# Sorted attention with a feed-forward block: the last three pairs' scatters and loads at other steps, pair 11 put back two rows a slot, and two other moves

## The chip, the cores and the metric

The kernel runs on one core of a Trainium2 chip. The metric is the device time of one execution in microseconds (us), and the number given for a kernel is the median of its runs. One execution of each kernel is profiled; its page and its trace show the engines TensorE (PE for matrix products, PEld for the loading of its weights), VectorE (DVE), ScalarE (ACT), GpSimd (POOL), and SyncE (SP), whose queue issues most of the DMAs ("SPq").

## The reference, cut to what matters

The inputs are `q`, `k` and `v` of 4 batches x 8 heads x 768 tokens x 64, and 16 centroids per head. Each query and each key belongs to the centroid it is most similar to, and a query sees only the keys of its own cluster. The result, with the heads side by side, is the input of a feed-forward block with 512 inputs and 2048 hidden features.

```python
q_assign = np.argmax(np.einsum('bhsd,hcd->bhsc', q_n, c_n), axis=-1)
k_assign = np.argmax(np.einsum('bhsd,hcd->bhsc', k_n, c_n), axis=-1)
mask = q_assign[:, :, :, None] == k_assign[:, :, None, :]
scores = np.where(mask, scale * np.matmul(q, k.transpose(0, 1, 3, 2)), -1e9)
attn = softmax(scores)
x = np.matmul(attn, v)            # then (B, H, S, D) -> (B*S, H*D)
h = x @ w_in
g = np.maximum(h, 0.0) + alpha * np.minimum(h, 0.0)
return g @ w_out
```

All is in float32.

## The kernel before

**Pairs, steps and slots.** Two heads are worked on together: 16 pairs `n`, four to a batch. Pairs 0 to 3 (n < `NCH` = 4) take the clusters into the scores by a second matmul; from pair 4 on a mask on DVE does it; and pairs 9 to 15 (n >= `NO` = 9) are sorted by cluster first ("ordered"), so that each chunk of 128 keys needs only a window of the queries. The program is written out by hand, in a fixed order, as a list of steps `u`. Each pair (or half of its queries) has three steps (`SB` = 3). A first loop runs to step 23 and a second from `TOGETHER` = 24 to step 75 (`NS`). In the second loop the pairs begin at these steps: 9 at 48, 10 at 51, 11 at 54, the two halves of pair 8 at 57 and 60, then 12 at 63, 13 at 66, 14 at 69 and 15 at 72. A step has five slots (`SLOTS`); in a first step of a pair the first three are taken by the two halves of its scores (L784 matmuls, exponentials L802 and L805) and by the weighing of the pair before (`weigh` L939, `weigh_near` L972), and only slots 3 and 4 are left.

**What fills a slot.** A slot issues, in this order: what `later` has put off to this tick (`tick`), one piece of the pair's own sums and masks (`mask` L825), possibly some scatters, then pieces of the feed-forward block of an earlier batch (`feed`), then what `prep_at` holds for the step and slot. A feed-forward piece is a hidden block of 128 features (`hidden`: L1066 matmuls, the copy L1072 on ACT, the slope L1058 on DVE, issued with the next piece) or a quarter of an output tile (`final`: L1084 matmuls; L1090, L1092 its end). Hidden and final products take their banks from `ps_f`, of two buffers; all small products share the one bank of `misc()`. The last batch's feed-forward block is another form, seven products in place of eight (`last_pieces`: `hidden` L1244, its copies L1176 and additions L1179, its `slopes` L1184; `final` L1300); there `g_sums` (L1223) and `w_out_sums` (L1232) form sums of the operands on DVE.

**The way of an ordered pair.**
- At step `ORDERS[n - NO]`, `load(n)` issues eight DMAs from `q` and `k` into two tiles of the pool `inp`, which has four buffers (`load_v`, L141, does the same for `v` of pairs that are not ordered). One and two steps later `order_features` (two transposes, L567) and `order_sims` (four matmuls, L575) follow, and behind these the counting on DVE (`order_counts`), `order_begins` (L601), `order_ranks` (L609 to L611) and `order_rows`, each put off by some ticks.
- `order_rows` puts the pair's scattering into the list `sorting`: six stages, each a load of 128 tokens of one head (`order_stage`, three DMAs on SP's queue, L661) and four scatters (`order_scatter`, an indirect DMA each on POOL's queue, L675, plus at the first of a stage a copy of token numbers). There are only two stage tiles, so that a stage's load waits until the scatters of the stage two before have read it. "13.2" is stage 2 of pair 13.
- How many scatters a slot issues is said by `scatters_at(v, s, i)`, where `v` is the step counted from 48. Ahead of them `pace` issues a token: a copy of one element on ACT (L651), which POOL reads by a copy (L652). So POOL keeps to the slots of ACT; tokens are in the pool `pace`, of eight buffers.
- `order_load(n)` reads the sorted pair back: two DMAs for the token numbers (L688), eight for queries and keys (L697), two for the values (L706), all on SP's queue. It stands in the program before the step of its start by a lead of 4, 3, 3, 4, 4, 4 and 3 steps for pairs 9 to 15.
- `prep_clusters` (L444, its copy L448) and `prep_keys` come four steps ahead of the pair's start, `order_blocks` (two transposes, L713) and `order_queries` (L719) in the step before it.
- Behind its last step: `invert` (L907) and `normalise_near` (L978). Then the result is turned to rows in two parts (`to_rows`, three transposes on PE, L1002, and a copy on ACT, L1005), and `put_back` scatters the 12 rows to their tokens, each with a token of `pace` (L1011). `fetch_back` reads the result (four DMAs on SP's queue, L1023) and `turn_back` (L1030, two transposes on DVE) puts it into the input of the feed-forward block. This is spread over slots: parts begin 6 and 12 ticks after `normalise_near`, a row a slot, and `turn_back` comes 7 ticks after `fetch_back`. Only pair 15 has its parts at 6 and 9, two rows a slot, and `turn_back` 4 ticks on.

**Queues.** Each engine, and SP as the issuer of DMAs, takes its instructions in the program's order. On SP's queue thus stand, one behind the other, `load`, `load_v`, `order_stage`, `order_load`, `fetch_back` and the stores of the output.

**The pairs 0 to 3.** `prep_argmax` leaves the clusters of a pair as rows of `member`, and `of_heads`, put off by 12 ticks for pair 0 and by 8 for the others, issues the copies for the second matmul: `prep_queries` (DMAs on ACT's queue, L476) and two activations (L431).

Of the kernel before, what the change touches and what calls it, by code (L numbers as in the profile page):

```python
# [23 lines left out]
def kernel(  # L24
# [70 lines left out]
    def later(slots, piece):  # L95
        due.setdefault(now[0] + slots, []).append(piece)
# [8 lines left out]
    NO = WHOLE * NCH - 3  # L105
    NP = len(pairs)
# [309 lines left out]
    def prep_argmax(n, ps):  # L416
        top, first, pieces = argmax(ps, exact=n < NCH)
        for piece in pieces:
            piece()
        firsts[n] = first  # L420
        if n >= NCH:
            return
        member = memp.tile([P, HS], BF16, name="member")
        outside = memp.tile([P, 2, HS], BF16, name="outside")
        nc.vector.transpose(out=member, in_=top.rearrange("p t c -> p (t c)"))

        def of_heads():
            if n > 0:
                prep_queries(n, 0, 0)
            for h in range(2):  # L430
                nc.scalar.activation(  # L431
                    out=outside[HP:P, h, :], in_=member[HP:P, :], func=AF.Identity,
                    scale=pick[HP:P, h:h + 1], bias=pick[HP:P, h + 2:h + 3])

        members[n] = member, outside
        later(12 if n == 0 else 8, of_heads)

    def prep_clusters(n):

# [286 lines left out]
    SB = NJ // GROUP  # L726
# [248 lines left out]
    def normalise_near(n):  # L975
        outT = inp.tile([P, 2, NJ, D], FP32, name="qk").rearrange("p h j d -> p (h j d)")
        for side in range(2):
            nc.vector.tensor_tensor(out=outT[:, side * HS:(side + 1) * HS],  # L978
                                    in0=pos.pop((n, side))[:, 0:HS],
                                    in1=rds.pop((n, side)), op=ALU.mult)  # L980
        whole = tc.dram_tile([2 * S, D], FP32, name=f"back{n}")
        to = dram_disjoint_views(whole, 2 * NJ)
        found = orders.pop(n)
        place = found[:, :, :, 0]
        nc.vector.tensor_scalar(out=place, in0=place, scalar1=0, scalar2=S - 1,
                                op0=ALU.max, op1=ALU.min)
        rows = [sorts["byrow"].tile([P, HJ, P], FP32, name=f"rows{i}") for i in range(2)]

        dense = n == NP - 1
        starts = (6, 9) if dense else (6, 12)  # L990
        for i in range(2):
            later(starts[i], lambda i=i: to_rows(outT, rows, i))
            for x in range(NJ):
                later(starts[i] + 2 + (x // 2 if dense else x),
                      lambda i=i, x=x: put_back(to, place, rows, i * NJ + x))
        later(starts[1] + 2 + (HJ if dense else NJ), lambda: fetch_back(n, whole))
# [19 lines left out]
    def fetch_back(n, whole):  # L1016

        b, hp = pairs[n]
        raw = inp.tile([P, 2, NJ, D], FP32, name="qk").rearrange("p h j d -> p (h j d)")
        for h in range(2):  # L1020
            for x in range(D // Q):
                r = h * D + x * Q
                nc.sync.dma_start(  # L1023
                    out=raw[r:r + Q, :].rearrange("p (t i) -> p t i", i=Q),
                    in_=whole[h * S:(h + 1) * S, x * Q:(x + 1) * Q].rearrange(
                        "(t p) i -> p t i", p=Q))

        def turn_back():
            for half in range(2):
                nc.vector.transpose(out=x_tile(b, half)[:, hp, :],  # L1030
                                    in_=raw[:, half * HS:(half + 1) * HS])
        later(4 if n == NP - 1 else 7, turn_back)

    def x_tile(b, half):
        if (b, half) not in xTs:
# [73 lines left out]
    KH, NQ, HC = NCH // 2, NF // 2, DM // 2  # L1109
# [32 lines left out]
    def last_pieces():  # L1142
# [75 lines left out]
        def g_sums(x):  # L1218
            (t0, t1), (z0, z1) = g[x][0], g[NQ + x][0]
            S1, S2, S4 = (g_sum(x, m) for m in ("S1", "S2", "S4"))  # L1220
            for to, p, q, op in ((S1, t1, z1, ALU.add), (S2, S1, t0, ALU.subtract),
                                 (t1, t0, t1, ALU.subtract), (S4, z0, S2, ALU.subtract)):
                nc.vector.tensor_tensor(out=to, in0=p, in1=q, op=op)  # L1223

        def w_out_sums(x):

            T1, T2, T3, T4 = (w_out_form(m, x) for m in ("T1", "T2", "T3", "T4"))
            B11, B12, B21, B22 = (
                w_out_sb[:, f, c0:c0 + HC].rearrange("p (a w) -> p a w", a=KH)
                for f in (x, NQ + x) for c0 in (0, HC))  # L1230
            for to, p, q in ((T1, B12, B11), (T2, B22, T1), (T3, B22, B12), (T4, B21, T2)):
                nc.vector.tensor_tensor(out=to, in0=p, in1=q, op=ALU.subtract)  # L1232

        late = deque()
# [101 lines left out]
            return [p1, p5, p6, p2, p7, p3, p4]  # L1336

        def room_for_y():
            late.popleft()()
            t = sorts["xmore"].tile([P, NCH, HS], FP32, name="xT").rearrange(  # L1340
                "p c q -> p (c q)")
            ys.extend(ypool.tile([P, DM], FP32, name="y") for _ in range(HJ))
            ys.extend(t[:, i * DM:(i + 1) * DM] for i in range(HJ))
            for x in (NQ - 2, NQ - 1):
                g_sums(x)
            for x in (NQ - 2, NQ - 1):
                w_out_sums(x)
        pieces = []
        for x in range(NQ):
            pieces += hidden(x)  # L1350
# [15 lines left out]
    FREE = SLOTS * SB - 3  # L1366


    ORDERS = [26, 29, 35, 38, 41, 56, 59]
    prep_at, load_at = {}, {}  # L1370
    for (n, half), u in start_of.items():
        def at(step, slot, piece):
            prep_at.setdefault((step, slot), []).append(piece)
        if half is None:
            t = ORDERS[n - NO]
            load_at.setdefault(t, []).append(lambda n=n: load(n))
            for i in range(2):
                at(t + 1, FIRST + i, lambda n=n, i=i: order_features(n, i))
            at(t + 2, 2, lambda n=n: order_sims(n))
            load_at.setdefault(u - (3 if n in (NO + 1, NO + 2, NP - 1) else 4), []).append(  # L1380
                lambda n=n: order_load(n))
            at(u - 4, 0, lambda n=n: prep_clusters(n))
            for i in range(2):
                at(u - 1, i, lambda n=n, i=i: order_blocks(n, i))
                at(u - 1, FIRST + i, lambda n=n, i=i: order_queries(n, i))
            continue
        if half == 0:
            if n < NCH:
                if n > 1:
                    load_at.setdefault(max(u - 7, 0), []).append(lambda n=n: load(n))  # L1390
                if n > 0:
                    load_at.setdefault(max(u - 6, 0), []).append(lambda n=n: load_v(n))
            else:
                load_at.setdefault(u - 9, []).append(lambda n=n: load(n))
                load_at.setdefault(u - 7, []).append(lambda n=n: load_v(n))
            if n < NCH:
                for g in range(len(groups)):
                    at(u - 4, FIRST + g, lambda n=n, g=g: prep_features(n, g))
            else:
                for w in range(2):  # L1400
                    at(u - 7, FIRST + w + (u - 7 == TOGETHER - 1),
                       lambda n=n, w=w: prep_blocks(n, w))
            at(u - (3 if n < NCH else 5 if u - 6 < TOGETHER else 6), FIRST,
               lambda n=n: prep_sims(n)) if u - 6 < 2 * TOGETHER else at(
                   u - 6, FIRST + 1, lambda n=n: prep_sims(n))
            if n >= NCH:
                at(u - 4, FIRST if u - 4 < TOGETHER else 0, lambda n=n: prep_clusters(n))
        if n < NCH:

            if half == 1 or n == 0:  # L1410
                at(u - (3 if half else 1), FIRST,
                   lambda n=n, half=half: prep_queries(n, half, 0))
            continue
        for h in range(2):
            at(u - 1, FIRST + h, lambda n=n, half=half, h=h: prep_queries(n, half, h))
# [4 lines left out]
    def scatters_at(v, s, i):  # L1420


        if v < SB:
            return 1 + (s == 0 or i == 0)
        if v < 3 * SB:
            return 0
        if v < 4 * SB:
            return int(s == 0 or i % 2 == 0)
        return 1 + (s == 0 or i % 2 == 0)

    def feed(pieces):
        for _ in range(pieces):
# [27 lines left out]
    for u in range(-AHEAD, TOGETHER):  # L1460
        for piece in load_at.get(u, []):
            piece()
        n, half, s = steps[max(u, 0)]
# [51 lines left out]
    for u in range(TOGETHER, NS + 1):  # L1515
        for piece in load_at.get(u, []):
            piece()
        if u < NS:
            n, half, s = steps[u]
        if s == 0 or u == NS:  # L1520
# [16 lines left out]
            if prior[1] is None:  # L1537
                normalise_near(prior[0])
            else:
                normalise(*prior)  # L1540
# [276 lines left out]
```

## Time and profile before

| what | value |
|---|---|
| median of three runs | 941.22 us |
| lowest and highest | 939.76 and 941.53 us |
| the profiled execution's own time | 941.51 us |
| its span in the trace | 939.6 us |
| mean granted clock of TensorE | 0.997 |
| matmuls, and instructions in all | 3963 and 11988 |
| L1066, hidden products of three batches | x768, 258.9 us, 490 ns each |
| L1084, final products of three batches | x576, 254.8 us, 596 ns each |
| L1011, rows put back | x84, 85.7 us, 1021 ns each |
| L1072, ACT's copies of hidden blocks | x96, 46.0 us, 479 ns each |

The span runs from the first to the last instruction; 1.9 us of the profiled execution's time lie around it. The page gives for each engine the time in which it was busy, and for each group of instructions its line, engine and tile, the count, the busy time and the mean of one, and then the engine's idle time just ahead of them with what ended most of it ("<-"). The busy time of the engines, stretch by stretch, of which the second loop is from 244 us on and the last batch's feed-forward block from about 750 us on:

| us of the span | PE | DVE | ACT | POOL | granted clock | DMA share |
|---|---|---|---|---|---|---|
| 0 to 100 | 94.03 | 74.97 | 59.70 | 31.07 | 1.00 | 0.50 |
| 100 to 244 | 144.00 | 125.38 | 51.06 | 25.65 | 1.00 | 0.54 |
| 244 to 440 | 195.39 | 157.00 | 49.85 | 114.56 | 1.00 | 0.33 |
| 440 to 545 | 100.75 | 85.75 | 31.20 | 70.19 | 0.98 | 0.53 |
| 545 to 662 | 113.42 | 82.67 | 27.52 | 86.78 | 1.00 | 0.53 |
| 662 to 750 | 88.00 | 45.69 | 18.75 | 32.81 | 1.00 | 0.18 |
| 750 to 860 | 109.35 | 68.86 | 19.72 | 21.21 | 1.00 | 0.08 |
| 860 to 940 | 74.14 | 15.86 | 4.96 | 0.00 | 0.98 | 0.06 |

### The profile page before, as it was taken

The numbers are of one execution on the slowest core, as the hardware profiler recorded it, in microseconds if no ns is written. First come the engines' busy times: TensorE is split into PE (matmuls) and PEld (weight loads), VectorE is DVE, ScalarE is ACT, GpSimd is POOL, SyncE is SP. The second block draws the span as 40 slices with busy tenths as digits, with TensorE's granted clock in tenths as the row PEclk, the third lists the DMA queues.
The fourth block names the chain that finished last, engine by engine and source line by source line (L and its number), as shares of the span: only waits on it lengthen the run. The fifth ranks groups of instructions, "written<-read, shape, count | busy, mean of one in ns | idle before, by whom it ended". The sixth has DMA issues, their size and how long they took to land.

```text
span 939.6 us, 11988 instructions
## 1 busy us (share of the span) xinstructions
PE 919.1 (98%) x3963; PEld 495.3 (53%) x3963; DVE 656.2 (70%) x1246; ACT 262.8 (28%) x661; POOL 382.3 (41%) x580
## 2 busy tenths in 40 slices
PE   8999999999999999999999999999999999999997
PEld 5534444445455454454544544555555555556886
DVE  5797798799679589598987889754647135598100
ACT  5764444323023132231212332122212120221000
POOL 2333222200026677478575786668533471000000
PEclk9999999999999999999999999999999999999999
DMA  8433758039002635252952383662501012000000
GB/s 298 135 117 98 144 131 150 18 62 196 1 9 72 156 82 137 62 120 76 176 100 41 59 138 73 149 124 60 92 31 27 12 37 53 1 0 1 23 23 25
DMA packets 226708, 77.71 MB, mean 83 GB/s; under 512 B 210752, under 2 KB 214544, under 8 KB 226640
## 3 DMA queue, kind: packets, MB, share of 16 engines
q1 hardware_dynamic: 217728, 62.72, 30.9%
q0 software_dynamic: 8064, 13.78, 4.7%
q8 instruction: 33, 0.54, 0.2%
q10 hardware_dynamic: 848, 0.39, 0.2%
q14 instruction: 35, 0.29, 0.1%
HBM read 52.25 MB, written 24.25 MB: 81 GB/s over the span
## 4 chain that ended last, share of the span: by engine, by line
PE 82%; DVE 10%; SPq 3%; DMA 1%; issue 1%; POOL 1%; ACT 1%; DVEq 0%; POOLq 0%; ACTq 0%
PE fps L1084 24%; PE fps L1066 22%; PE sps L784 6%; PE vps L939 5%; PE sps L1244 4%; PE sps L1300 4%; PE vps L1244 2%; PE vps L1300 2%; PE fps L784 2%; SPq L697 1%; PE mps L972 1%; PE fps L1300 1%; PE fps L1244 1%; PE vps L972 1%; SPq L127 1%
## 5 line engine op out<-in xcount | busy, mean ns | idle before, releaser
L1066 PE MATMUL fps<-xT,w_in_sb 128*128 128x384 f32 x768 | 258.9, 490 | 0.0
L1084 PE MATMUL fps<-w_out_sb,gT 128*128 128x512 f32 x576 | 254.8, 596 | 2.5 <-DVE gT L1058 2.5
L675 POOL DMA_INDIRECT scratch<-stage,off x168 | 177.9, 1059 | 75.1 <-issue 29.6
L1066 PEld LDWEIGHTS fps<-xT,w_in_sb 128*128 128x128 f32 x768 | 142.5, 190 | 103.1 <-issue 4.3
L1084 PEld LDWEIGHTS fps<-w_out_sb,gT 128*128 128x128 f32 x576 | 107.4, 190 | 134.8 <-issue 121.4
L1072 ACT COPY gT<-fps 128x384 f32<-128x384 f32 x96 | 46.0, 479 | 236.2 <-PE fps L1066 236.2
L652 POOL COPY paced<-pace 1x1 f32<-1x1 f32 x205 | 51.2, 250 | 139.5 <-ACT pace L651 138.9
L1058 DVE SCALAR_TENSOR_TENSOR gT<-gT,alpha 128x384 f32<-128x384 f32 x96 | 61.2, 647 | 58.7 <-ACT gT L1072 58.5
L1011 POOL DMA_INDIRECT back<-rows,off x84 | 85.7, 1021 | 24.2 <-issue 18.6
L784 PE MATMUL sps<-qkT 64*128 64x384 f32 (+1 forms) x464 | 86.1, 490 | 0.4 <-DVE qkT L713 0.4
L805 ACT ACTIVATE E<-sps 128x768 f32<-128x768 f32 (+1 forms) x76 | 56.3, 786 | 62.6 <-PE sps L793 38.4
L784 PEld LDWEIGHTS sps<-qkT 64*128 64x128 f32 x464 | 41.8, 188 | 39.7 <-issue 14.6
L825 DVE SCALAR_TENSOR_TENSOR more<-aq,key,more 128x384 f32<-128x384 bf16 (+2 forms) x116 | 60.4, 577 | 0.0
L939 PE MATMUL vps<-E,vt 128*64 128x384 f32 x292 | 54.2, 495 | 1.5 <-DVE xT L1042 1.5
L271 POOL TENSOR_TENSOR w_in_sb<-w_in_sb,power 128x512 f32<-128x512 f32 x16 | 25.7, 1612 | 68.6 <-DVE w_in_sb L268 68.6
L825 DVE SCALAR_TENSOR_TENSOR E<-aq,key,E 128x384 f32<-128x384 bf16 (+2 forms) x88 | 45.3, 569 | 0.6 <-ACT E L802 0.6
L271 POOL TENSOR_TENSOR w_out_sb<-w_out_sb,power 128x512 f32<-128x512 f32 x16 | 22.5, 1412 | 56.0 <-DVE w_out_sb L268 56.0
L907 DVE RECIPROCAL inverses<-mps 64x12 f32<-64x12 f32 (+1 forms) x42 | 10.5, 249 | 48.1 <-PE mps L894 47.9
L835 DVE TENSOR_TENSOR acc<-acc,E 128x768 f32<-128x768 f32 x35 | 33.3, 951 | 14.6 <-ACT E L805 13.6
L1090 ACT COPY y<-fps 128x512 f32<-128x512 f32 x18 | 10.6, 587 | 102.3 <-PE fps L1084 102.3
L1092 DVE TENSOR_TENSOR y<-y,fps 128x512 f32<-128x512 f32 x24 | 16.3, 680 | 28.5 <-PE fps L1084 28.5
L805 ACT ACTIVATE more<-sps 128x768 f32<-128x768 f32 (+1 forms) x40 | 29.2, 764 | 12.5 <-PE sps L784 11.6
(284 smaller groups left out, 1178.4 us busy)
## 6 DMA issues: line engine op xcount, KB each, us to landing
raw<-in_moe_w_in_dram SPq DMA_DIRECT2D x16, 512.0 KB
raw<-in_moe_w_out_dram SPq DMA_DIRECT2D x16, 512.0 KB
out_dram<-y SPq DMA_DIRECT2D x21, 256.0 KB
qk<-scratch SPq DMA_DIRECT2D x56, 96.0 KB
qk<-in_q_dram SPq DMA_DIRECT2D x48, 96.0 KB
qk<-in_k_dram SPq DMA_DIRECT2D x48, 96.0 KB
w_in_kept<-w_in_sb SPq DMA_DIRECT2D x8, 512.0 KB
vt<-in_v_dram SPq DMA_DIRECT2D x9, 384.0 KB
```

What stands on the lines that cost most here:

```text
L652: nc.gpsimd.tensor_copy(out=sorts["paced"], in_=token)
L675: nc.gpsimd.indirect_dma_start(out=scratch[n][1][h * NX + xx], out_offset=bass.IndirectOffsetOnAxis(ap=ranks[n][:, xx, h:h + 1], axis=0), ...
L784: nc.tensor.matmul(out=bank(ps, h, m), lhsT=qkT[r:r + D, S + c * P:S + (c + 1) * P], rhs=qkT[r:r + D, tokens], start=True, stop=not early_ ...
L805: nc.scalar.activation(out=E[:, :, 0:m], in_=ps[:, :, 0:m], func=AF.Exp, scale=SCALE)
L825: nc.vector.scalar_tensor_tensor(out=e, in0=of, scalar=keys[n][:, NJ + c, h:h + 1], in1=e, op0=ALU.is_equal, op1=ALU.mult)
L939: nc.tensor.matmul(out=po[r:r + D, 0:HS], lhsT=vts[n][:, h, c, :], rhs=e[:, h, :], start=(c == 0), stop=(c == NJ - 1))
L1011: nc.gpsimd.indirect_dma_start(out=to[i], out_offset=bass.IndirectOffsetOnAxis(ap=place[:, h, j:j + 1], axis=0), in_=rows[j // HJ][:, j % ...
L1058: nc.vector.scalar_tensor_tensor(out=gs[f], in0=gs[f], scalar=alpha[:, f:f + 1], in1=gs[f], op0=ALU.mult, op1=ALU.max)
L1066: nc.tensor.matmul(out=ps[:, 0:HS], lhsT=w_in_sb[:, c, f * P:(f + 1) * P], rhs=xTs[b, half][:, c, :], start=(c == 0), stop=(c == NCH - 1))
L1084: nc.tensor.matmul(out=ps[:, 0:DM], lhsT=gs[f][:, i * P:(i + 1) * P], rhs=w_out_sb[:, f, :], start=on and f == f0, stop=off and f == f0 + ...
L1244: nc.tensor.matmul(out=bank[to], lhsT=w_in_form(m, x, cc), rhs=rhs[:, cc, :], start=start and cc == 0, stop=cc == KH - 1, skip_group_check ...
L1300: nc.tensor.matmul(out=bank[to], lhsT=g_form(m, x, t), rhs=w_out_form(n, x), start=start and x == 0, stop=x == NQ - 1, skip_group_check=no ...
```

## The change

Five things are moved; no instruction is added or taken away but tokens of `pace`, whose number follows the number of slots that scatter.

1. `of_heads` of pairs 1 to 3 is put off by 9 ticks, not 8.
2. Pair 11 (`NO + 2`) is put back as pair 15 is, two rows a slot: its parts begin 5 and 8 ticks after `normalise_near`, and its `turn_back` comes 4 ticks after `fetch_back`.
3. In the last batch's feed-forward block, `room_for_y` leaves the postponed product `p4` in the list `late`, and puts the sums for the last `x` behind it, so that both are issued after the first product of `final(0)`.
4. `ORDERS`: pair 14 is ordered at step 55 (was 56) and pair 15 at 60 (was 59). The leads of `order_load` are now a list, 4, 3, 3, 3, 3, 2, 2: the loads of pairs 12, 13, 14 and 15 stand at steps 60, 63, 67 and 70 (were 59, 62, 65 and 69).
5. `scatters_at`: the slots scatter up to step 49 (was 50); none do in steps 50 to 59 (was 51 to 56, and in 57 to 59 every slot of a first step and every second slot of the others did); from step 60 as before, and from step 66 two in each slot.

```diff
--- before.py
+++ after.py
@@ -433,7 +433,7 @@
                     scale=pick[HP:P, h:h + 1], bias=pick[HP:P, h + 2:h + 3])
 
         members[n] = member, outside
-        later(12 if n == 0 else 8, of_heads)
+        later(12 if n == 0 else 9, of_heads)
 
     def prep_clusters(n):
 
@@ -986,8 +986,8 @@
                                 op0=ALU.max, op1=ALU.min)
         rows = [sorts["byrow"].tile([P, HJ, P], FP32, name=f"rows{i}") for i in range(2)]
 
-        dense = n == NP - 1
-        starts = (6, 9) if dense else (6, 12)
+        dense = n in (NO + 2, NP - 1)
+        starts = {NO + 2: (5, 8), NP - 1: (6, 9)}.get(n, (6, 12))
         for i in range(2):
             later(starts[i], lambda i=i: to_rows(outT, rows, i))
             for x in range(NJ):
@@ -1029,7 +1029,7 @@
             for half in range(2):
                 nc.vector.transpose(out=x_tile(b, half)[:, hp, :],
                                     in_=raw[:, half * HS:(half + 1) * HS])
-        later(4 if n == NP - 1 else 7, turn_back)
+        later(4 if n in (NO + 2, NP - 1) else 7, turn_back)
 
     def x_tile(b, half):
         if (b, half) not in xTs:
@@ -1336,15 +1336,13 @@
             return [p1, p5, p6, p2, p7, p3, p4]
 
         def room_for_y():
-            late.popleft()()
             t = sorts["xmore"].tile([P, NCH, HS], FP32, name="xT").rearrange(
                 "p c q -> p (c q)")
             ys.extend(ypool.tile([P, DM], FP32, name="y") for _ in range(HJ))
             ys.extend(t[:, i * DM:(i + 1) * DM] for i in range(HJ))
-            for x in (NQ - 2, NQ - 1):
-                g_sums(x)
-            for x in (NQ - 2, NQ - 1):
-                w_out_sums(x)
+            g_sums(NQ - 2)
+            w_out_sums(NQ - 2)
+            late.append(lambda: (g_sums(NQ - 1), w_out_sums(NQ - 1)))
         pieces = []
         for x in range(NQ):
             pieces += hidden(x)
@@ -1366,7 +1364,8 @@
     FREE = SLOTS * SB - 3
 
 
-    ORDERS = [26, 29, 35, 38, 41, 56, 59]
+    ORDERS = [26, 29, 35, 38, 41, 55, 60]
+    LEADS = [4, 3, 3, 3, 3, 2, 2]
     prep_at, load_at = {}, {}
     for (n, half), u in start_of.items():
         def at(step, slot, piece):
@@ -1377,7 +1376,7 @@
             for i in range(2):
                 at(t + 1, FIRST + i, lambda n=n, i=i: order_features(n, i))
             at(t + 2, 2, lambda n=n: order_sims(n))
-            load_at.setdefault(u - (3 if n in (NO + 1, NO + 2, NP - 1) else 4), []).append(
+            load_at.setdefault(u - LEADS[n - NO], []).append(
                 lambda n=n: order_load(n))
             at(u - 4, 0, lambda n=n: prep_clusters(n))
             for i in range(2):
@@ -1420,13 +1419,11 @@
     def scatters_at(v, s, i):
 
 
-        if v < SB:
+        if v < SB - 1:
             return 1 + (s == 0 or i == 0)
-        if v < 3 * SB:
+        if v < 4 * SB:
             return 0
-        if v < 4 * SB:
-            return int(s == 0 or i % 2 == 0)
-        return 1 + (s == 0 or i % 2 == 0)
+        return 1 + (s == 0 or i % 2 == 0 or v >= 6 * SB)
 
     def feed(pieces):
         for _ in range(pieces):
```

## Prediction

> **What bounds the kernel now.** First the page's busy table and costliest groups:
>
> ```profile
> PE 919.1 (98%) x3963; PEld 495.3 (53%) x3963; DVE 656.2 (70%) x1246; ACT 262.8 (28%) x661; POOL 382.3 (41%) x580
> ...
> L675 POOL DMA_INDIRECT scratch<-stage,off x168 | 177.9, 1059 | 75.1 <-issue 29.6
> ...
> L652 POOL COPY paced<-pace 1x1 f32<-1x1 f32 x205 | 51.2, 250 | 139.5 <-ACT pace L651 138.9
> ```
>
> TensorE (PE) is the bound: 919.1 of 939.6 us, so all that can be won anywhere is 20.5 us, and a change of order acts through PE's gaps alone. POOL's 41% is an average; what counts is whether its scatters are in time for the loads behind them. Second, PE's own waits, those that the change can touch:
>
> ```profile
> PE fps L1084 <- DVE gT L1058: 2.5, 2, 2.3
> ...
> PE mps L575 <- issue: 1.3, 1, 1.3
> ...
> PE mps L575 <- ACT rows L1005: 1.1, 1, 1.1
> ...
> PE sps L1244 <- DVE gT L1179: 0.6, 1, 0.6
> ```
>
> One is large, 2.3 us. Third, the timeline around it, all engines:
>
> ```profile
> 482.36 4.61 SPq L697 DMA_DIRECT2D qk<-scratch  x8
> ...
> 487.35 0.98 DVE L713 STREAM_TRANSPOSE qkT<-qk 128x768 f32<-128x768 f32 x1 [1.44 <-DMA qk<-scratch]
> ...
> 490.13 0.98 DVE L713 STREAM_TRANSPOSE qkT<-qk 128x768 f32<-128x768 f32 x1 [1.80 <-DMA qk<-scratch]
> ...
> 491.45 1.14 DVE L1058 SCALAR_TENSOR_TENSOR gT<-gT,alpha 128x384 f32<-128x384 f32 x2
> ...
> 492.11 2.59 PE L1084 MATMUL fps<-w_out_sb,gT 128*128 128x512 f32 x4 [2.29 <-DVE gT L1058]
> ```
>
> VectorE (DVE) waits for the ordered rows of pair 11, the slopes (L1058) queue behind it, PE waits for them. Right after the gap the granted clock in the trace is half for 3.41 us (windows: 0.96 in 486 to 494, 0.94 in 494 to 517). Fourth, why the rows were late, SyncE's queue before that:
>
> ```profile
> 466.33 0.39 SPq L141 DMA_DIRECT2D vt<-in_v_dram  x1
> 472.92 0.61 SPq L661 DMA_DIRECT2D stage<-in_q_dram  x1
> ...
> 479.09 0.60 SPq L661 DMA_DIRECT2D stage<-in_q_dram  x1
> ...
> 481.06 1.20 SPq L688 DMA_DIRECT2D off<-scratch  x2
> ```
>
> Two stage loads of pair 13 stand ahead of pair 11's load, each waiting for scatters. Fifth, ScalarE's (ACT) waits in 500 to 760:
>
> ```profile
> ACT pace L651 <- POOL paced L652: 5.0, 2, 2.6
> ```
>
> The pace tokens have 8 buffers: ACT can be only eight tokens ahead of POOL, then it stops, and with it the copies that PE needs. It stopped twice, while POOL was some 22 us late around step 62; PE did not pay.
>
> [...] here 3.41 us at 0.5 after a gap of 2.29 us, none after gaps up to 1.48 us. [...] here scatter to landing is 2.2 to 4.0, median 2.6 us in 590 to 660, and 2.2 us when little else moves.
>
> **The change, part by part** (all times on the old trace's clock; a step's start is its first L784 matmul: 57 at 517.4, 60 at 544.2, 63 at 575.9, 66 at 621.4, 69 at 661.4, 72 at 702.9).
>
> Scatters pause at step 50: 7 scatters and 2 stage loads (3 DMAs each) leave the queue ahead of pair 11's load. It can issue after 466.7, takes 7.3 us as before, and has landed by about 477; its buffers were free at 460. The two transposes then start at 485.9, where DVE now begins to wait, keys and slopes are done by 488.8, PE asks at 489.8. So the gap goes with its half clock: 2.29 + 3.41/2 = **4.0 us**. Cover is 1.0 us; without it up to that much returns.
>
> Last pieces: the postponed p4 no longer waits for the addition before it (0.65 us gap); 16 matmuls of the first final product (3.45 us) come between. DVE's sums for the last x end about 869, their first user reaches them at 870.5. **-0.7 us.**
>
> The heads' mask one tick later: -1.5 to +1.0 us (the L356 wait of 1.5 us stands beside it; the aq DMAs for pair 3 land just as PE uses them). I take 0.
>
> Pair 14's ordering one step sooner: its two transposes (0.97 us each) fall into DVE's idle 2.9 us before 516.3; its load's 8 DMAs now stand ahead of fetch_back 9, whose rows land at 511.4 anyway: nothing. PE's sims wait for pair 11's normalising (0.65 us) in place of the rows (1.06). Pair 11's second rows copy now stops the cluster matmuls as those rows did (+1.06), the begin and sims waits after step 60 (0.3 and 1.3) go: about -1.2. The put-back's reading, next, takes that away again, so I take 0 for both together (-2 to +3).
>
> Pair 11 put back two rows a slot: 12 rows start near 536 at POOL's own rate (pair 15 in the old trace: 12 tokens and rows from 759.9 to 777.8, 1.49 us each, at best 1.32). With 1.35: last row placed 552, landed 553.5. fetch_back 2.1 us and 2.4 us to land: 558. DVE comes to turn_back 11 near 553 and stands 5 us, where it stood 2.6 us for pair 15's load before. Queued behind: masks, the slopes of pieces 14 and 15. They end near 566.8 (565.1 before), PE wants them at 562.6 to 565.2: 1.6 to 2.2 us.
>
> The later scatters, the costly part. Now SP's queue is, in order: fetch_back 11, order_load 12 (7.5 us, as at 617.8 to 625.4), load 15 (5.7 us, as at 548.9 to 554.5), then stage 13.2 (1.9 us to issue, 2 to land): 553.5 + 2.1 + 7.5 + 5.7 + 3.9 = **572.7** for the scatter that the plan puts at 557. A scatter with its share of token and index copy is 1.385 us (603.2 to 625.3: 16 scatters). Pair 13's other 16: 594.9. Then order_load 13 must see the last landing (1.3 us after its end) and issues ahead of stage 14.0: 1.3 + 7.5 + 3.9 = 12.7 us in which POOL has nothing; before, loads came two steps later and POOL had the next pair's rows. Pair 14's 24: 607.6 to 640.8; again 12.7: pair 15 begins at **653.5**, where the plan wants it at 630 and the old kernel began at about 612. From there POOL owes two scatters (2.68) and one row of pair 12 (1.32) a slot, 4.0 us against PE's 2.6. ACT's token at step 69 slot 4 needs the eighth before it read: nine pairs of scatters (24.1) and five rows (6.6) after 653.5, 684.2. In the old trace that token went at 669.5. Hidden piece 15's copy stands behind it: copy 0.5, slope 0.6, and the last matmuls (0.9) end at 686.4, not 678.1: +8.2 us on PE. The same steps laid along the old order put the last scatter of pair 15 at 653.3, the trace has it at 654.6, 1.3 later; I add it: **+9.5 us**, between -2 (POOL in time) and +14 (rows at 1.49 us, DMA under load). Earlier waits of PE are inside this, since POOL's chain sets the time. Order_load 15 then lands about 710, just as PE, 9 us late, reaches 72; nothing more.
>
> Sum against the profiled execution's 941.5: - 4.0 - 0.7 + 9.5 = 946.3; it is 0.3 above the median of 941.2: **946.0**.
>
> **Rivals.**
> (a) POOL in time, faster. The mechanism is the eight-token stop at steps 68 to 69: it costs nothing if pair 15's first scatter starts before about 645, as PE's slack at that token is then not used. For it: the old trace had POOL 22 us late without harm. Against: there PE had the score pieces in which to catch up; two 12.7 us holes now follow. Time: 941.2 - 4.7 = 936.5.
> (b) As (a), but DVE's stand at turn_back 11 is the new stall: 2.2 us and a half clock of 1.7: 940.4.
> (c) The gap at 492 stays (order_load 11 held by a buffer, not by the stage loads) and POOL is late: 950. Against: the buffers' last readers end at 460.
> (d) POOL late by the upper bound, with half clocks at its stops: 952.
>
> **Chances.** Main case 0.55, (a) 0.25, (b) and what lies between 0.12, (c) and (d) 0.08. About 0.2% (1.9 us) is what can be told from no change. The main case's own range is 943 to 950.5. Its lower edge and (b) touch the same-band: faster 0.27, same 0.12, slower 0.61. Range for 8 in 10: 936.0 to 951.0; below lie half of (a)'s luck, above (d).
>
> **What would show it.** Right: no PE gap and no half clock near 490; the SP queue going from pair 10's loads to pair 11's without stage loads; POOL idle near 557 to 572, 595 to 607, 641 to 653, before scatters that wait for stage loads; ACT's wait for POOL at L651 grown from 5 to some 20 us or more; PE gaps in steps 68 to 70 behind ACT's copies. Wrong: POOL's holes under 8 us, or ACT's wait unchanged; then 936 to 940. If PE's gaps lie at 560 to 575 instead, it was DVE's stand.

## The result and the profile after

The changed kernel takes **963.15 us** (median of six runs, 961.03 to 966.39) where the kernel before takes 940.77 (six runs, 939.76 to 941.53): a ratio of **1.0242**, 95% interval 1.0223 to 1.0261. It is 22 us slower, where 5 us slower was forecast. The span of its profile is 961.5 us at a mean clock of 0.992. A first set of four experiments ran where the kernel before itself took 950.5 us and ACT and DVE stood idle for up to 18 us with nothing of the program to wait for: the pause alone came to 1.0154 there, `turn_back` with step 59 to 1.0359, the four places to 1.0121; these three were run again, with the results below, and of that set only the kernel of the last pieces is used.

First the busy table and the costliest groups of the changed kernel's page:

```profile
PE 927.2 (96%) x3963; PEld 498.1 (52%) x3963; DVE 656.6 (68%) x1246; ACT 263.2 (27%) x654; POOL 380.3 (40%) x573
...
L675 POOL DMA_INDIRECT scratch<-stage,off x168 | 176.4, 1050 | 104.0 <-DMA stage<-in_v_dram 47.3
```

The work is the same; 8 us more of PE's busy time is matmuls that took longer (three more stretches of 3.41 us at half rate, a granted clock of 0.5, make up to 5 of them, by estimate), the other 14 are gaps. The scatters' idle time is now ended by stage loads (47.3 us), not by POOL's own issue. PE's waits in the changed kernel (us in total, times, longest):

```profile
PE fps L1066 <- ACT gT L1072: 5.4, 2, 2.9
PE mps L972 <- DVE inverses L907: 4.7, 2, 3.7
PE fps L1084 <- DVE gT L1058: 4.0, 4, 1.9
PE sps L793 <- ACT outside L431: 2.6, 3, 1.9
PE sps L784 <- DVE qkT L713: 2.1, 2, 1.6
...
PE fps L1300 <- DVE gT L1184: 1.4, 1, 1.4
```

The one large wait of before, 2.3 us, has become several. To see where they lie, take the first L784 matmul of each pair in both traces (of step 75, which has no scores, the first L972) and subtract; the differences add up to the two spans' 21.8 us:

| stretch | before, us | after, us | difference | the prediction |
|---|---|---|---|---|
| start to step 48 | 438.5 | 441.6 | +3.1 | 0 |
| 48 to 57 | 78.9 | 74.8 | -4.1 | -4.0 |
| 57 to 63 | 58.5 | 64.3 | +5.7 | 0 (a stand of 2, held to be inside the later term) |
| 63 to 66 | 45.5 | 44.6 | -0.9 | 0 |
| 66 to the end of 74 | 125.8 | 143.8 | +18.1 | +9.5 |
| 75 to the end | 192.5 | 192.4 | -0.1 | -0.7 |

**Steps 48 to 57: as forecast.** SyncE's queue of the changed kernel, and then all engines, where the gap had been:

```profile
469.50 0.39 SPq L141 DMA_DIRECT2D vt<-in_v_dram  x1
469.94 2.27 SPq L688 DMA_DIRECT2D off<-scratch  x2
```

```profile
487.69 7.03 PE L1084 MATMUL fps<-w_out_sb,gT 128*128 128x512 f32 x16
...
488.99 1.83 DVE L713 STREAM_TRANSPOSE qkT<-qk 128x768 f32<-128x768 f32 x2
```

No stage load stands between the load of `v` and pair 11's load, its transposes wait for no DMA, and PE runs 16 final matmuls without a gap.

**Steps 9 to 11, on which nothing was forecast.** All engines around pair 3's masks:

```profile
62.61 1.29 ACT L431 ACTIVATE outside<-member,pick 64x384 bf16<-64x384 bf16 x2 [0.68 <-DMA raw<-in_moe_w_out_dram]
...
63.37 0.93 PE L793 MATMUL sps<-aq,outside 32*128 32x384 bf16 x4 [1.85 <-ACT outside L431]
```

With `of_heads` a tick later, ACT runs the two L431 (62.61 us) only after PE's L784 of the step (59.95 to 61.51); before, it ran them at 58.93, ahead of L784 at 59.29. PE waits 1.85 us and soon after runs at half rate (granted clock 0.83 in 60 to 70 us). From the first scores (13.53 and 14.20 us) to those of step 11 it is 55.60 us before and 58.00 after, 2.4 more; the other 0.67 lies ahead of the first scores.

**Steps 57 to 63.**

```profile
554.65 2.06 SPq L1023 DMA_DIRECT2D qk<-back  x4
...
559.24 1.04 DVE L1030 STREAM_TRANSPOSE xT<-qk 128x384 f32<-128x384 f32 x2 [6.46 <-DMA qk<-back]
...
564.30 3.36 SPq L127 DMA_DIRECT2D qk<-in_q_dram  x4
564.38 1.12 PE L1084 MATMUL fps<-w_out_sb,gT 128*128 128x512 f32 x2 [1.93 <-DVE gT L1058]
...
570.42 0.64 SPq L661 DMA_DIRECT2D stage<-in_q_dram  x1
...
574.95 1.30 POOL L675 DMA_INDIRECT scratch<-stage,off  x1 [14.98 <-DMA stage<-in_v_dram]
```

The chain of the prediction is here, 1 to 2 us later than forecast (rows landed 558, scatter 13.2 at 572.7): `fetch_back` 11, `order_load` 12, load 15, stage 13.2. DVE stands 6.46 us at `turn_back` 11, the slopes behind it are late, PE waits twice (1.93, and 1.33 at 566.83) and then runs at half rate (granted clock 0.83 in 562 to 572).

**Steps 66 to 74.** Pair 14's last scatter has run at 645.29; its load and the beginning of pair 15:

```profile
648.71 4.57 SPq L697 DMA_DIRECT2D qk<-scratch  x8
...
654.66 0.63 SPq L661 DMA_DIRECT2D stage<-in_q_dram  x1
...
659.97 0.97 POOL L675 DMA_INDIRECT scratch<-stage,off  x1 [13.42 <-DMA stage<-in_v_dram]
...
662.40 0.19 ACT L651 COPY pace<-ones 1x1 f32<-1x1 f32 x1 [7.20 <-POOL paced L652]
662.50 0.46 ACT L1072 COPY gT<-fps 128x384 f32<-128x384 f32 x1
...
663.02 2.85 PE L1066 MATMUL fps<-xT,w_in_sb 128*128 128x384 f32 x8 [2.86 <-ACT gT L1072]
```

and its end, ahead of step 72:

```profile
707.12 0.96 POOL L675 DMA_INDIRECT scratch<-stage,off  x1 [0.30 <-issue]
...
715.54 0.98 DVE L713 STREAM_TRANSPOSE qkT<-qk 128x768 f32<-128x768 f32 x1 [6.68 <-DMA qk<-scratch]
...
718.22 0.98 DVE L713 STREAM_TRANSPOSE qkT<-qk 128x768 f32<-128x768 f32 x1 [1.70 <-DMA qk<-scratch]
...
722.75 1.04 DVE L1030 STREAM_TRANSPOSE xT<-qk 128x384 f32<-128x384 f32 x2 [2.17 <-DMA qk<-back]
...
726.89 1.55 PE L972 MATMUL mps<-more,vt 128*64 128x384 f32 x4 [3.74 <-DVE inverses L907]
```

The holes on POOL are there (14.98, 13.64 at 611, 13.42 us; forecast were 12.7 for the last two), and ACT's wait at L651 in 500 to 760 has grown from 5.0 to 41.0 us. What the prediction had not: pair 15's rows reach DVE at 715 to 718, PE still waits 0.47 us for them ahead of step 72 (719.25), and 3.74 us inside it. There `fetch_back` 12 is late as well, behind POOL's late rows and behind load 15 on SP's queue (issued at 716.58); DVE stands 2.17 us at `turn_back` 12, and L907, for which PE waits, comes behind it. Of the 18.1 us, 12.5 lie ahead of step 72 and 5.6 in it.

### The profile page after: what moved, and what is told of

It reads as the page before. It is cut to its first block, busy times and chain, and to the rows that moved or that the text cites. A ratio compares the mean times of both kernels' runs of the same rounds, so it can differ in the third digit from the quotient of the medians.

```text
span 961.5 us, 11966 instructions
## 1 busy us (share of the span) xinstructions
PE 927.2 (96%) x3963; PEld 498.1 (52%) x3963; DVE 656.6 (68%) x1246; ACT 263.2 (27%) x654; POOL 380.3 (40%) x573
## 4 chain that ended last, share of the span: by engine, by line
PE 72%; DVE 8%; POOL 6%; DMA 5%; SPq 4%; issue 3%; ACT 1%; POOLq 0%; ACTq 0%; DVEq 0%
PE fps L1084 19%; PE fps L1066 19%; PE vps L939 6%; PE sps L784 6%; PE sps L1244 4%; PE sps L1300 4%; POOL scratch L675 3%; PE vps L1244 2%; PE vps L1300 2%; POOL back L1011 2%; PE fps L784 2%; SPq L697 2%; DMA scratch<-stage,off 1%; PE fps L1244 1%; PE mps L972 1%
## 5 line engine op out<-in xcount | busy, mean ns | idle before, releaser
L1066 PE MATMUL fps<-xT,w_in_sb 128*128 128x384 f32 x768 | 261.0, 493 | 6.4 <-ACT gT L1072 5.4
L675 POOL DMA_INDIRECT scratch<-stage,off x168 | 176.4, 1050 | 104.0 <-DMA stage<-in_v_dram 47.3
L1066 PEld LDWEIGHTS fps<-xT,w_in_sb 128*128 128x128 f32 x768 | 143.2, 191 | 111.1 <-ACT gT L1072 6.9
L784 PE MATMUL sps<-qkT 64*128 64x384 f32 (+1 forms) x464 | 85.1, 485 | 2.1 <-DVE qkT L713 2.1
L784 PEld LDWEIGHTS sps<-qkT 64*128 64x128 f32 x464 | 41.3, 186 | 40.9 <-issue 12.9
L939 PE MATMUL vps<-E,vt 128*64 128x384 f32 x292 | 55.6, 505 | 0.0
L907 DVE RECIPROCAL inverses<-mps 64x12 f32<-64x12 f32 (+1 forms) x42 | 10.5, 251 | 48.1 <-PE mps L894 38.0
L651 ACT COPY pace<-ones 1x1 f32<-1x1 f32 x198 | 28.3, 185 | 49.2 <-POOL paced L652 49.2
```

The lines of the kernel that those rows point to most:

```text
L675: nc.gpsimd.indirect_dma_start(out=scratch[n][1][h * NX + xx], out_offset=bass.IndirectOffsetOnAxis(ap=ranks[n][:, xx, h:h + 1], axis=0), ...
L784: nc.tensor.matmul(out=bank(ps, h, m), lhsT=qkT[r:r + D, S + c * P:S + (c + 1) * P], rhs=qkT[r:r + D, tokens], start=True, stop=not early_ ...
L939: nc.tensor.matmul(out=po[r:r + D, 0:HS], lhsT=vts[n][:, h, c, :], rhs=e[:, h, :], start=(c == 0), stop=(c == NJ - 1))
L1066: nc.tensor.matmul(out=ps[:, 0:HS], lhsT=w_in_sb[:, c, f * P:(f + 1) * P], rhs=xTs[b, half][:, c, :], start=(c == 0), stop=(c == NCH - 1))
```

## The experiments

Theory A: the losses are three and lie apart: POOL's holes behind `order_load` 13 and 14, which reach PE through the landing of pair 15's load as much as through the tokens; the crowd on SP's queue at step 60; and `of_heads`. Theory B: the eight-token stop is the mechanism, as forecast.

**More tokens.** The changed kernel with

```diff
-                           ("xmore", 1), ("byrow", 1), ("pace", 8)):
+                           ("xmore", 1), ("byrow", 1), ("pace", 16)):
```

> The changed kernel (963.15 us) with 16 buffers for the pace tokens in place of 8. Theory A (POOL's own lateness sets the end, the tokens are only one of its two ways to TensorE): ACT's wait for POOL at L651, 41 us in 500 to 780, falls below 15 us and the PE gaps at 663 to 684 go, but pair 15's last scatter still runs at about 707 and its rows still land at about 717, so PE waits ahead of step 72 instead: 960 to 963 us. Theory B (the eight-token stop is the mechanism, as the prediction had it): the 12.4 us lost in steps 66 to 71 come back and load 15 is no bound: 945 to 952 us.

1.0220 to the kernel before (1.0204 to 1.0235), where the changed kernel has 1.0242. The waits of PE, and of ACT in 500 to 760:

```profile
PE sps L784 <- DVE qkT L713: 13.8, 2, 12.6
```

```profile
ACT pace L651 <- POOL paced L652: 2.7, 2, 2.0
```

ACT no longer stops, PE's three gaps at 663 to 676 are gone, and PE waits 12.6 us ahead of step 72 instead, which begins at 719.3 us in both kernels. So theory B, that the tokens alone set the time, falls: in the changed kernel the stops for tokens and the landing of pair 15's load hold step 72 to within 0.5 us of the same time, and taking the first away only moves the wait.

**The loads a slot later.** The changed kernel with `order_load` of pairs 13 and 14 behind the first two stage loads of the next pair:

```diff
-            load_at.setdefault(u - LEADS[n - NO], []).append(
-                lambda n=n: order_load(n))
+            t, load_now = u - LEADS[n - NO], lambda n=n: order_load(n)
+            if n in (NO + 4, NO + 5):
+                at(t, 3 if t % SB == 0 else 0, load_now)
+            else:
+                load_at.setdefault(t, []).append(load_now)
```

> The changed kernel with order_load of pairs 13 and 14 issued one slot later in the program, behind the first two stage loads of the next pair on SP's queue. Theory A (the two holes of 13.4 us on POOL come from the stage loads standing behind order_load): both holes shrink below 5 us, pair 15's first scatter moves from 660 to about 640 us, the PE gaps at 663 to 684 and at 719 to 730 go: 963.15 less 12.4 less 5.6, about 945 us. Theory C (POOL is late because two scatters a slot at 1.39 us are more than a slot's 2.6 us, and the holes only add to it): at most 5 us back, 958 or more.

1.0072 (1.0057 to 1.0088): 0.0170 of 941, **16.0 us**, come back. Steps 66 to 74 take 127.8 us, not 143.8. Its SyncE queue at pair 13's load, and POOL's waits in 500 to 760:

```profile
599.67 0.59 SPq L661 DMA_DIRECT2D stage<-in_q_dram  x1
...
601.63 1.20 SPq L688 DMA_DIRECT2D off<-scratch  x2
```

```profile
POOL scratch L675 <- DMA stage<-in_v_dram: 23.3, 3, 15.1
```

The stage load is now ahead of the load that waits. Of POOL's three waits for stage loads the longest, 15.1 us, is the one at step 60, which this kernel leaves; the other two are 8.2 us together. Pair 15's first scatter runs at 642.2 us, not 660.0, and PE's waits at 663 to 684 are gone. Theory C (two scatters a slot are too many as such) falls: POOL is in time as soon as it is fed.

**Pair 11's turn_back, alone and with pair 15's load.** The first kernel puts `turn_back` back to 7 ticks, the second puts pair 15's step back to 59 as well:

```diff
-        later(4 if n in (NO + 2, NP - 1) else 7, turn_back)
+        later(4 if n == NP - 1 else 7, turn_back)
...
-    ORDERS = [26, 29, 35, 38, 41, 55, 60]
+    ORDERS = [26, 29, 35, 38, 41, 55, 59]
```

> The changed kernel with pair 11's turn_back 7 ticks after fetch_back, as before, in place of 4. Theory A (DVE's stand of 6.5 us at turn_back 11 costs PE its two gaps at 564 and 567, the half clock behind them and the 1.6 us ahead of step 63): the step 60 to 63 shortens by some 4.8 us and the end by as much: about 958.4 us. Theory D (what the prediction said: POOL's later chain sets the time, and earlier waits of PE are inside it): no change, 962 to 964 us.

> The changed kernel with pair 11's turn_back at 7 ticks and pair 15's load and ordering at step 59, a second time for the same reason. Theory A (the two bounds of steps 60 to 62 are DVE's stand at turn_back 11 and the late load of pair 15; both go): step 60 to step 63 in 31.5 to 32.5 us as before, not 36.6, and a ratio to the kernel before of 1.0242 less 0.005, 1.019. Theory F (a third wait takes their place): 36 us again, 1.023 to 1.025. Theory D (step 63 sooner, but POOL's chain sets step 72): 1.023 to 1.025.

Alone: 1.0237 (1.0223 to 1.0251), no change, theory A's 4.8 us missed. The trace says why:

```profile
571.24 0.98 DVE L567 STREAM_TRANSPOSE qk<-qk 128x768 f32<-128x768 f32 x1 [7.55 <-DMA qk<-in_q_dram]
...
572.32 1.09 PE L575 MATMUL mps<-qk,cT 128*32 128x384 f32 x4 [3.41 <-DVE qk L567]
```

The stand at `turn_back` is gone, and DVE stands as long for pair 15's load, which lies behind the same `fetch_back` 11 and `order_load` 12 on SP's queue; its sims then hold PE. With both undone it is 1.0172 (1.0155 to 1.0188), 6.6 us less by the ratio and 4.1 by the spans. Steps 57 to 62 take 56.6 us, not 64.3 (60 to 62 take 28.9, less than theory A's 31.5); of these 7.7 us steps 66 to 74 take 3.5 back (147.3 for 143.8), since POOL's holes are still there. So theory D holds for the half of it: the waits of step 60 are real, but part of their price was hidden under the later ones.

**The heads' mask.** The changed kernel with 8 ticks:

```diff
-        later(12 if n == 0 else 9, of_heads)
+        later(12 if n == 0 else 8, of_heads)
```

> The changed kernel with of_heads 8 ticks later, as before, in place of 9. Theory A (the two L431 activations of pair 3 stand behind the aq DMAs on ACT, PE waits 1.9 us at 63.4 and runs at half clock): steps 9 to 12 shorten by 2.4 us and the end by as much: about 960.7 us. Theory D (later waits swallow it, or the 1.5 us gap at 67.7 of the kernel before returns in full): 962 to 964 us.

1.0216 (1.0197 to 1.0234), 2.4 us less than 1.0242; the two intervals overlap, but the traces decide: from the first scores to those of step 11 it is 55.54 us where the changed kernel has 58.00, and PE's wait for L431 falls from 2.6 to 0.8 us. From the first scores to step 48 the five traces with 8 ticks in this document's table below take 425.0 us, the five with 9 ticks 427.4 to 427.9.

**The pause alone.** The kernel before, with the scatters that step 50 loses put into steps 57 to 59 (six are lost, and eight more find room there):

```diff
-        if v < SB:
+        if v < SB - 1:
...
-            return int(s == 0 or i % 2 == 0)
+            return 1 + (s == 0 or i == 0)
```

> The kernel before with the scatters' pause one step sooner alone, a second time (the first profile had idle stretches of up to 14 us on ACT and DVE with their inputs ready, and the kernel before was 1% slower than elsewhere beside it, so its time told nothing). Theory A (the stage loads ahead of order_load 11 make the gap at 492): no PE gap and no half clock near 490, a ratio of 0.9957. Theory B (POOL's eight further scatters in steps 57 to 59 take it back): the gap is gone and a later one is there, a ratio of 0.999 to 1.004.

1.0058 (1.0041 to 1.0075): theory B, and somewhat worse than its range. Steps 48 to 56 take 75.3 us, 3.6 less than before, so the gain is the pause's. But POOL gets eight scatters more beside pair 11's rows, and here the eight-token stop does hold PE (ACT's waits at L651 in 500 to 760 are 21.9 us, 5.0 in the kernel before):

```profile
547.54 0.19 ACT L651 COPY pace<-ones 1x1 f32<-1x1 f32 x1 [0.62 <-POOL paced L652]
547.64 0.46 ACT L1072 COPY gT<-fps 128x384 f32<-128x384 f32 x1
...
548.16 1.65 PE L784 MATMUL fps<-qkT 64*128 64x384 f32 x2 [4.70 <-ACT gT L1072]
```

ACT comes to the copy late, PE has no free bank for pair 8's scores, and steps 57 to 62 take 65.9 us in place of 58.5. The scatters of the pause can't go just anywhere later.

**The last pieces alone.** The kernel before with `room_for_y` of the changed one:

```diff
-            late.popleft()()
...
-            for x in (NQ - 2, NQ - 1):
-                g_sums(x)
-            for x in (NQ - 2, NQ - 1):
-                w_out_sums(x)
+            g_sums(NQ - 2)
+            w_out_sums(NQ - 2)
+            late.append(lambda: (g_sums(NQ - 1), w_out_sums(NQ - 1)))
```

> The kernel before with the change in room_for_y alone (p4 and the last x's sums behind the first product of the last final). Prediction's step: the gap of 0.65 us ahead of p4 at 860 goes and nothing follows: 0.7 us less, a ratio of 0.9993. Theory E, from the changed kernel's trace: the slopes of the postponed p4 (L1184) are now late for a later product, with a gap of 1.4 us near 868: 0.65 less, 1.4 more, and 0.7 us slower: a ratio of 1.0007.

1.0015 (1.0002 to 1.0028), theory E's side: PE waits 1.4 us for L1184, where it had waited 0.65 for L1179. This is of the first set; from step 75 to the end its trace takes 193.0 us, the kernel before 192.5.

**The three causes undone together, and two more moves.** The first kernel joins the edits of `of_heads`, `turn_back`, step 59 and the two loads; the pause, pair 11's dense rows, pair 14's step and the other leads stay as changed. The second also takes back `room_for_y` and gives `turn_back` of pair 12 ten ticks:

```diff
-        later(4 if n == NP - 1 else 7, turn_back)
+        later(4 if n == NP - 1 else 10 if n == NO + 3 else 7, turn_back)
```

> The changed kernel with the four places undone together (of_heads 8, turn_back 7, pair 15's load at step 59, order_load 13 and 14 a slot later), a second time for the same reason. If the losses are the three that theory A names: 1.0242 less 0.017 (holes), 0.0026 (of_heads) and 0.005 (steps 60 to 62), about 0.9996; with the 3 us at steps 72 to 75 that the kernel with the loads behind still had, up to 1.002. If a fourth cause is in it: over 1.004.

> The kernel with the four places undone together, and two more moves: pair 12's turn_back 10 ticks after fetch_back in place of 7 (only this pair's), and room_for_y as before. There PE waited 3.2 us at 704 for L907, which stood on DVE behind turn_back 12 (DVE idle 2.35 us for the rows) and the slopes; and 1.4 us at 866 for L1184, where the kernel before had waited 0.65. If these are the causes: 2.2 and 0.75 us less, a ratio to the kernel before of 0.9958 less 0.0031, 0.9927. If order_blocks and order_queries of pair 15, late with its load, hold L907 anyway: only the 0.75, 0.995.

The first is at **0.9958** (0.9944 to 0.9971), better than the 0.9996 that the single sums gave. That fits the half of step 60's price that was hidden before and is now won too (3.5 us, where 0.0038 is 3.6), and no further cause of that size is needed. A smaller one is left, in step 72:

```profile
700.06 1.04 DVE L1030 STREAM_TRANSPOSE xT<-qk 128x384 f32<-128x384 f32 x2 [2.35 <-DMA qk<-back]
...
704.20 0.87 PE L972 MATMUL mps<-more,vt 128*64 128x384 f32 x4 [3.20 <-DVE inverses L907]
```

The second is at **0.9927** (0.9913 to 0.9940; 935.67 us beside 942.6), as expected: 6.9 us faster than the kernel before. In it DVE doesn't stand at `turn_back` 12, and of PE's waits for L907 only one of 1.3 us at 466.9 is left:

```profile
PE mps L972 <- DVE inverses L907: 1.3, 1, 1.3
```

The steps from one pair's first scores to another's, in all these kernels (75 by its first L972; the kernel of the last pieces, of the first set, is left out):

| kernel | ratio to before | 57 to 63, us | 66 to 75, us |
|---|---|---|---|
| before | 1 | 58.5 | 125.8 |
| changed | 1.0242 | 64.3 | 143.8 |
| 16 tokens | 1.0220 | 64.2 | 142.2 |
| loads a slot later | 1.0072 | 64.2 | 127.8 |
| turn_back at 7 | 1.0237 | 64.9 | 144.8 |
| turn_back at 7, pair 15 at 59 | 1.0172 | 56.6 | 147.3 |
| heads' mask at 8 | 1.0216 | 65.0 | 143.9 |
| before with the pause | 1.0058 | 65.9 | 125.8 |
| four places undone | 0.9958 | 56.6 | 129.2 |
| and two more moves | 0.9927 | 56.6 | 125.8 |

## Why the prediction was wrong, step by step

- **The pause, -4.0 us: right.** -4.1 us in the changed kernel, -3.6 alone, by the mechanism named (with one small miscount: step 50 loses six scatters, not seven). But 1.7 of the 4.0 is the half rate behind the gap (half of the 3.41 us), and a longer gap can come without it: in the changed kernel, the eight L1066 matmuls behind a gap of 2.86 us at 663.0 took 2.85 us, at a granted clock of 1.00.
- **The heads' mask, taken as 0 between -1.5 and +1.0: wrong, +2.4.** The working looked at when the DMAs of pair 3 land, not at the two L431 that stand behind them on ACT; and it allowed for no half rate behind a gap of 1.85 us. The wait that it names, L356's, stands at 45 us in both traces; the one that goes is L939's of 1.47 us at 67.7.
- **Last pieces, -0.7: no gain.** The wait moved from L1179 (0.65) to the postponed product's slopes L1184 (1.4). Alone the change came to +1.4 us by the ratio and +0.5 by the traces, in the first set; between the traces of before and after this stretch differs by 0.1 us, so a loss is likely and its size is open.
- **Pair 14 sooner and pair 11 dense, 0 together: wrong, +5.7.** The stand was forecast at 5 us and was 6.46; its price on PE was put at 1.6 to 2.2 us and then dropped, in the sentence "Earlier waits of PE are inside this, since POOL's chain sets the time". Only 3.5 of 7.7 us were inside. With the crowd on SP's queue gone, steps 57 to 62 take 56.6 us, 1.9 less than before; PE's wait of 1.34 us ahead of L575 at 560 is gone there, as the working had it for the sooner ordering of pair 14, but that move was not tested alone.
- **The later scatters, +9.5: the cause right, the term mis-sized, +18.1**, beyond its upper end of 14. The holes were right to a microsecond (13.64 and 13.42 for 12.7), and pair 15's first scatter came at 660 for 653.5. PE's waits at the tokens were right too, 8.1 us in all (2.86, 2.55, 1.72 and 0.99) for 8.2; the half rate behind them (granted clock 0.89 in 660 to 675) was not counted. The step that failed is "Order_load 15 then lands about 710, just as PE, 9 us late, reaches 72; nothing more". The rows reached DVE at 715.5 and 718.2; the same lateness that stops PE at the tokens reaches it a second time at this load and at what stands behind it, so that without the token stops it costs PE 12.6 us there, and with them still 5.6 us inside step 72. Most of it stood in the forecast's own numbers: 653.5 and twelve slots of 4.0 us make 701.5 for pair 15's last scatter, and a load of 7.5 us behind its landing some 710, for two transposes on DVE that must be done before a step then due at about 708 (702.9 less 4.0, plus 9.5).
- **Rivals:** (a) POOL in time, and (b), a stand at `turn_back`, were forecast faster; POOL was not in time, and the stand was real but came on top. The condition of (a), a first scatter of pair 15 before about 645, held where it was met: at 642.2 us, with the loads a slot later, PE's stops at 663 to 684 were gone. (d), POOL later with half clocks, at 952, was the nearest, and had 0.08 with (c).

What stays open: the hole at step 60 (14.98 us) falls to 7.95 us with load 15 at step 59, but what it costs PE by itself was not measured, and no kernel put pair 11's rows back one a slot.

## What to carry to other kernels

When one late engine can stop the bound engine at two places, price both and take the later: lengthening the buffer of the first (16 tokens for 8) only moved the wait. SP's queue issued in the program's order here: in the changed kernel pair 13's load waited 8.2 us in it for a scatter, until 598.9 us, and pair 14's first stage load was issued behind it, at 606.9. In such a queue, place a load that waits for the end of one item behind the loads that start the next; two loads moved by one slot were worth 16 us here. A move that wins (the pause, 4 us) says nothing on the moves that make room for it; cost the instructions behind each moved one on every engine, two activations behind a DMA issue included.

## What the runs showed of the hardware

Half rate does not follow from the length of PE's gap alone. Gaps of 2.29 us (before, at 492.1), 2.55 us (changed, 668.4) and 3.74 us (changed, 726.9) came with a granted clock of 0.5 for 3.41 us, and one of 1.85 us (changed, 63.4) had the same soon behind it; after 2.86 us (changed, 663.0) and 3.20 us (four places undone, 704.2) the clock stayed full. The matmuls just behind the gaps took:

| kernel, gap | matmuls | us | granted clock |
|---|---|---|---|
| changed, 2.86 us at 663.0 | L1066 x8 | 2.85 | 1.00 |
| changed, 2.55 us at 668.4 | L1066 x8 | 4.54 | 0.62 |
| four places undone, 3.20 us at 704.2 | L972 x4 | 0.87 | 0.999 over the whole span |
| changed, 3.74 us at 726.9 | L972 x4 | 1.55 | 0.50 |

The prediction took its two observations, half rate after 2.29 us and none after gaps up to 1.48, for a matter of the gap's length. The gaps here are against that: 1.85 us had half rate behind it, 2.86 and 3.20 us did not. What else decides was not shown.
